# One PSUM tile of two banks for the scores and for the value sums of a unit, with one instruction each for what reads them

## The chip, the cores and the metric

The kernel runs on one core of a Trainium2 chip. The metric is device time in microseconds (us), lower is better. Several runs are made of each kernel and the median is compared. An engine executes its own queue in order: PE is TensorE (matmul), PEld its weight loads, DVE is VectorE, ACT ScalarE, POOL GpSimd, SP the queue that issues most stores and the transposing DMAs. TensorE writes only to PSUM, which has eight banks of 512 fp32 columns; DVE and ACT read it from there.

## The reference

Attention over a sliding window of 32 positions to each side, then a two-layer network with a sigmoid-approximated gelu:

```
scores = (1 / sqrt(64)) * q @ k^T            # q, k, v: (8 batches, 8 heads, 576 positions, 64)
scores = where(|i - j| <= 32, scores, -1e9)
attn   = exp(scores - max) / (sum + 1e-9)
x      = (attn @ v), heads side by side       # 4608 tokens x 512
h      = x @ w_in                             # 512 x 2048
out    = (h * sigmoid(1.702 * h)) @ w_out     # 2048 x 512
```

## The kernel before

**Units and windows.** The 4608 tokens are cut into 36 units of 128. For a unit `u`, `scores(u)` makes transposed scores (keys on partitions, queries on the free axis) of eight heads as two tiles of 128x512, `sc0` for the even heads and `sc1` for the odd ones; each tile is one PSUM bank. Two exponentials (line 277) turn them into the bf16 tile `p`, 128 x (2 x 512). `band(u)` multiplies each half of `p` by a 0/1 mask of the sliding window on DVE (line 288). `values(u)` multiplies `p` (as weights) with `v` and a column of ones, four heads to a bank, so that column 64 of each head is the sum of its exponentials; `norm(u)` then takes, for each bank, four reciprocals (line 310) and one product (line 311) into `x`. `x_T(u)` transposes `x` into `xT`, by a DMA in SP's queue or, in the head, by TensorE.

`layer1(t, d)` does a pair of 128-wide slices of the first layer for two units (256 tokens), eight matmuls into one bank and a gelu on ACT. The second layer is written as seven `product`s of eight matmuls, as in Strassen's method, with sums of `g` (`g_sums`) and of the weights (`w_sums`), and `keep` and `result` moving or adding partial results.

`head()` handles the first seven units with an order of its own. `window(w)` for w = 4 to 17 takes units a = 2w and b = 2w + 1 through attention, layer 1 of the window before, and layer 2 of the window before that. `close()` ends w = 18 and 19. All queues follow the order in which the calls stand (a manual schedule): an instruction placed after another on its engine runs after it.

**PSUM.** All banks come from one pool by tag (`bank`, line 61): "h" has two buffers, "o" one, "t" one, and "a" four, together eight banks. The buffers of a tag are given out in turn; the first write to one waits for the last reader of the tile that held it. "a" serves scores and values, and in the head and in `close` also the transposes `rows_T` and `x_T`, one layer 1 tile, filler matmuls (`keep_busy`) and partial sums of layer 2. `blind(u)` writes an additive mask into the score tiles of units 0 to 3 by matmul, so these need no `band`.

**The part of a window that the change touches** (lines 664 to 672): `product(5)`, `band(a)`, `product(6)`, `band(b, 0)`, `keep(6)`, `band(b, 1)`, one `layer1`, `values(a)`, `values(b)`. On DVE that is: two mask products of a, one of b, the copy of `keep(6)` (line 105, `part<-o_ps`), which waits for `product(6)`, and the second mask product of b. On TensorE: product 5, product 6, eight matmuls of layer 1, 16 matmuls of `values(a)` and 16 of `values(b)`. `norm(a)` and `x_T(a)` follow on DVE and SP.

Of the kernel before, what the change touches and what calls it, by code (L numbers as in the profile page):

```python
# [15 lines left out]
F32 = mybir.dt.float32  # L16
BF16 = mybir.dt.bfloat16
F16 = mybir.dt.float16
AF = mybir.ActivationFunctionType
ALU = mybir.AluOpType  # L20

SQ = 64
# [5 lines left out]
class _Kernel:  # L28
# [30 lines left out]
        self.gs, self.part, self.o_sb = {}, {}, {}  # L59

    def bank(self, kind, shape, dtype, name):
        bufs = {"h": 2, "o": 1, "a": 4, "t": 1}[kind]
        return self.ps.tile(shape, dtype, name=name, tag=kind, bufs=bufs)


    def setup(self):
# [162 lines left out]
    def setup_neg(self):  # L229
# [12 lines left out]
        for rows, b in ((lo, 0), (hi, 1)):  # L242
# [2 lines left out]
            dve.tensor_scalar(out=self.neg[rows, 1 - b, :], in0=tri[0][rows, pad:], scalar1=30000.0, scalar2=-30000.0,  # L245
                              op0=ALU.mult, op1=ALU.add)

    def blind(self, u):

        sc = self.sc[u] = [self.bank("a", [128, 8, SQ], F32, f"sc{eo}") for eo in range(2)]  # L250
        neg = self.neg.rearrange("k (o b) s -> k o b s", o=1).to_broadcast([128, 4, 2, SQ])
        for eo in range(2):
            self.nc.tensor.matmul(sc[eo].rearrange("k (h b) s -> k h b s", b=2), self.ident, neg,
                                  start=True, stop=False, skip_group_check=True)

    def scores(self, u):
        nc = self.nc
        seen = u not in self.sc
        if seen:
            self.sc[u] = [self.bank("a", [128, 8, SQ], F32, f"sc{eo}") for eo in range(2)]  # L260
        sc = self.sc.pop(u)
        k0, q0 = 128 * u % RING, (128 * u + 32) % RING
        for hp in range(4):
            for chunks in ((1, 0), (2,)):
                for eo in range(2):
                    r = slice(eo * 64, eo * 64 + 64)
                    for c in chunks:
                        lo = 64 * (c % 2)
                        b0, n = (1, 1) if c == 2 else (0, 1 + c)
                        nc.tensor.matmul(sc[eo][lo:lo + 64, 2 * hp + b0:2 * hp + b0 + n, :],  # L270
                                         self.kT[r, hp, k0 + 64 * c:k0 + 64 * c + 64],
                                         self.qT[r, hp, q0 + SQ * b0:q0 + SQ * (b0 + n)],
                                         start=(seen and hp == 0 and c < 2), stop=(hp == 3 and c > 0),
                                         skip_group_check=not seen)
        p = self.work.tile([128, 2, 8, SQ], BF16, name="p", tag="p", bufs=5)
        for eo in range(2):
            nc.scalar.activation(p[:, eo], sc[eo], AF.Exp, scale=self.scale)  # L277
        self.p[u] = p

    def band(self, u, only=None):  # L280

        p = self.p[u]
        cross = [(2 * u + i) % 9 == 8 for i in range(2)]
        a, b = 0 if cross[0] else 1, 2 if cross[1] else 3
        for eo in range(2) if only is None else (only,):
            pv = p[:, eo].rearrange("p (h b) s -> p h b s", b=2)
            msk = self.mask[:, a:b + 1:b - a, :].rearrange("p (o b) s -> p o b s", o=1)
            self.nc.vector.tensor_mul(pv, pv, msk.to_broadcast([128, 4, 2, SQ]))  # L288

    def values(self, u, kinds="aa"):  # L290
        nc, D = self.nc, self.D
        p = self.p.pop(u)
        acc = [self.bank(kinds[i], [128, 4, D + 1], F32, f"pv{i}") for i in range(2)]
        for half in range(2):
            for hh in range(4):
                h = 4 * half + hh
                for blk in range(2):
                    vt = (self.ve, self.vo)[blk][u % NV]
                    nc.tensor.matmul(acc[half][blk * 64:blk * 64 + 64, hh, :], p[:, h % 2, h // 2 * 2 + blk, :],  # L299
                                     vt[:, h, :D + 1], start=(hh == 0), stop=(hh == 3))  # L300
        self.acc[u] = acc

    def norm(self, u):
        nc, D = self.nc, self.D
        acc = self.acc.pop(u)
        x = self.work.tile([128, self.H, D], BF16, name="x", tag="x", bufs=4)
        rec = self.work.tile([128, self.H, 1], F32, name="rec", tag="rec", bufs=3)
        for half in range(2):
            hs = slice(4 * half, 4 * half + 4)
            nc.vector.reciprocal(rec[:, hs, :], acc[half][:, :, D:D + 1])  # L310
            nc.vector.tensor_mul(x[:, hs, :], acc[half][:, :, :D], rec[:, hs, :].to_broadcast([128, 4, D]))  # L311
        self.x[u] = x
# [285 lines left out]
    def window(self, w):  # L598
        nc, dve, sp = self.nc, self.nc.vector, self.nc.sync
        a, b = 2 * w, 2 * w + 1  # L600
        att = w < self.NW
        t, act = w - 2, nc.scalar
        l1 = [(lambda d=d: self.layer1(w - 1, d)) for d in range(8)] if w <= self.NW else []

        def run(lst, n=1):
            for _ in range(min(n, len(lst))):
                lst.pop(0)()

        def loads():
            for m in (2 * w + 6, 2 * w + 7):  # L610
                if m < self.NU:
                    self.load_v(m)
            i, chunks = w // 2 + 2, ((0, 1), (2, 3))[w % 2]
            if 512 * i < self.N:
                for c in "kq":
                    self.load_rows(c, i, chunks)

        if w == 4:
            l2 = [(lambda u=u, i=i: self.layer2(u, i, "oh"[u % 2], (dve, act)[u % 2])) for u in (4, 5) for i in range(4)]
            self.scores(7)  # L620
            self.scores(a)
            run(l2, 3)
            self.band(7)
            self.scores(b)
            run(l2)
            self.band(a)
            self.values(7, "th")
            self.gelu_table()
            self.band(b)
            self.norm(7)  # L630
            run(l2, 2)
            self.values(a)
            self.values(b)
            run(l2)
            self.x_T(7, "t", nc.scalar)
            self.norm(a)
            self.x_T(a)
            self.norm(b)
            self.x_T(b)
            run(l2)  # L640
            loads()
            for m in (10, 11):
                self.odd_v(m, dve)
            run(l1, 8)
            self.g_sums(w - 1, 0)
            self.feed(w)
            return
        loads()
        if not att:
            self.close(w, l1)  # L650
            return
        self.scores(a)
        if w > 5:
            self.scores(b)
        self.g_sums(t, 1, (0, 1))
        self.product(t, 1, "o")
        self.keep(t, 1, dve)
        self.product(t, 2, "h")
        if w == 5:
            self.scores(b)  # L660
        self.g_sums(t, 1, (2, 3))
        self.result(t, 11)
        self.gelu_table()
        self.product(t, 5, "t")
        self.band(a)
        self.product(t, 6)
        self.band(b, 0)
        self.keep(t, 6, dve)
        self.band(b, 1)
        run(l1)  # L670
        self.values(a)
        self.values(b)
        self.norm(a)
        self.x_T(a)
        self.product(t, 7)
        self.keep(t, 7, dve)
        self.result(t, 22)
        run(l1, 1)
        self.product(t, 4)
        self.result(t, 21, act)  # L680
        self.norm(b)
        self.x_T(b)
        self.product(t, 3)
        self.result(t, 12)
        run(l1, len(l1) - 4)
        self.g_sums(w - 1, 0)
        self.feed(w)
        run(l1, 4)
# [104 lines left out]
```

The softmax here doesn't subtract the row's maximum and nothing guards it: scores larger than these inputs give would overflow.

## Time and profile before

| | |
|---|---|
| median of four runs | 292.23 us (291.64 to 293.12) |
| the profiled execution | 293.12 us, of which 291.4 us are the span of its instructions |
| busy: PE, DVE, ACT, POOL | 283.5, 192.7, 183.4, 101.8 us |
| granted TensorE clock | 1.0 |
| first-layer matmuls (line 339) | 1152, 134.9 us busy (they overlap) |
| exponentials of 128x512 (line 277) | 72, 604 ns each |
| mask products of 128x512 bf16 (line 288) | 64, 424 ns each |
| reciprocals of 128x4 (line 310) | 72, 174 ns each |
| norm products of 128x256 from PSUM (line 311) | 72, 424 ns each |
| one window in the steady state | 14.57 us |

A line of the table of groups gives the source line, the engine, the operation, output and inputs by their names in the program, the shapes, the count, then the busy time in us and the mean in ns of one; after the second bar stands the idle time of the engine just before such instructions and what ended most of it. A line of the timeline gives start and length in us, then the same names; neighbours of one kind are merged ("x8"). Ends of matmuls are modelled, so that the starts of TensorE's instructions say more than its busy time.

### The profile page before, as it was taken

Reading aid. Unit: us, or ns where it says so; the run is one execution under the profiler, and the core shown is the slowest. Engines: PE = TensorE matmul, PEld = TensorE weight load, DVE = VectorE, ACT = ScalarE, POOL = GpSimd, SP = SyncE. Lnnn points to the kernel's source line nnn. Section 1 sums busy time; section 2 is a strip of 40 time slices with the busy share of each in tenths; the row PEclk is TensorE's granted clock in tenths of the full one; section 3 lists DMA queues with packets and bytes.
Section 4 is the critical chain, followed back from the end, with each engine's and each line's share of the span. In section 5 each row is a group of like instructions: output and inputs, shape, how many; then the busy total and the mean of one; then the engine's idle time right before and its main releaser. Section 6 shows DMA issues by size and latency. Waiting matters only on the chain.

```text
span 291.4 us, 9011 instructions
## 1 busy us (share of the span) xinstructions
PE 283.5 (97%) x3757; PEld 234.0 (80%) x3759; DVE 192.7 (66%) x563; ACT 183.4 (63%) x301; POOL 101.8 (35%) x140
## 2 busy tenths in 40 slices
PE   7979999999999999999999999999999999999995
PEld 3658765866888888888888888888888888888884
DVE  6762467699575858585858585858585858583352
ACT  4566557685766766676767676767676767675330
POOL 8845424998624443433333434332000000000000
PEclk9999999999999999999999999999999999999999
DMA  9999999999999999999999999999935230303012
GB/s 149 180 196 206 199 183 150 172 143 174 177 138 148 156 158 156 144 155 170 134 170 123 155 132 152 141 156 135 158 66 145 38 94 18 97 18 94 2 72 72
DMA packets 144824, 38.79 MB, mean 133 GB/s; under 512 B 129936, under 2 KB 140432, under 8 KB 144784
## 3 DMA queue, kind: packets, MB, share of 16 engines
q0 software_dynamic: 97232, 18.16, 84.6%
q1 hardware_dynamic: 47104, 19.67, 39.1%
q8 instruction: 29, 0.48, 0.7%
q10 hardware_dynamic: 448, 0.39, 0.5%
q14 instruction: 11, 0.09, 0.1%
HBM read 36.96 MB, written 9.44 MB: 159 GB/s over the span
## 4 chain that ended last, share of the span: by engine, by line
PE 88%; DMA 9%; POOL 1%; DVE 1%; issue 0%; ACT 0%; POOLq 0%; DVEq 0%
PE h_ps L339 41%; PE o_ps L401 31%; PE o_ps L351 7%; PE pv L299 4%; PE sc L270 3%; DMA xT<-x 3%; DMA w_in_sb<-in_moe_w_in_dram 3%; DMA ve<-in_v_dram 2%; PE tp L178 1%; POOL ve L159 1%; PE tp L326 0%; DVE o_sb L419 0%; POOL ks L137 0%; POOL qs L137 0%; DVE part L105 0%
## 5 line engine op out<-in xcount | busy, mean ns | idle before, releaser
L339 PE MATMUL h_ps<-xT,w_in_sb 128*128 128x256 bf16 x1152 | 134.9, 273 | 1.3 <-DMA w_in_sb<-in_moe_w_in_dram 1.0
L341 ACT ACTIVATE g<-h_ps 128x512 f16<-128x512 f32 x144 | 85.6, 595 | 74.9 <-PE h_ps L339 73.4
L339 PEld LDWEIGHTS <-w_in_sb 128*128 128x128 bf16 x1152 | 112.1, 98 | 15.1 <-DMA w_in_sb<-in_moe_w_in_dram 1.2
L159 POOL DMA_DIRECT2D ve<-in_v_dram x41 | 34.5, 858 | 82.0 <-PE pv L299 63.6
L401 PEld LDWEIGHTS <-gs 128*128 128x128 f16 x480 | 45.8, 98 | 5.8
L401 PE MATMUL o_ps<-w_sum,gs 128*128 128x256 f16 x360 | 44.3, 273 | 0.0
L277 ACT ACTIVATE p<-sc 128x512 bf16<-128x512 f32 x72 | 37.2, 604 | 3.3 <-PE sc L270 3.1
L378 DVE TENSOR_TENSOR gs<-g 128x512 f16<-128x512 f16 x30 | 12.8, 425 | 38.4 <-ACT g L341 38.4
L401 PEld LDWEIGHTS <-g 128*128 128x128 f16 x360 | 34.2, 98 | 4.5 <-ACT g L341 0.2
L311 DVE TENSOR_TENSOR x<-pv,rec 128x256 bf16<-128x256 f32 x72 | 30.6, 424 | 2.5
L401 PE MATMUL o_ps<-w_out_sb,g 128*128 128x256 f16 x240 | 29.1, 273 | 0.0
L105 DVE COPY vo<-ve 64x528 bf16<-64x528 bf16 x71 | 24.5, 346 | 4.7 <-DMA ve<-in_v_dram 3.1
L105 DVE COPY part<-o_ps 128x256 f32<-128x256 f32 x45 | 19.1, 424 | 12.2 <-PE o_ps L401 11.1
L419 DVE TENSOR_TENSOR o_sb<-o_ps,part 128x256 f32<-128x256 f32 x45 | 19.0, 422 | 12.1 <-PE o_ps L401 11.4
L288 DVE TENSOR_TENSOR p<-p,mask 128x512 bf16<-128x512 bf16 x64 | 24.6, 424 | 0.0
L147 POOL DMA_DIRECT2D qs<-in_q_dram x27 | 23.2, 885 | 3.6 <-DMA ks<-in_k_dram 1.7
L351 PE MATMUL o_ps<-w_out_sb,g 128*128 128x512 f16 x96 | 23.2, 380 | 0.0
L147 POOL DMA_DIRECT2D ks<-in_k_dram x27 | 23.0, 882 | 0.3 <-issue 0.3
L438 ACT ACT_TABLE_LOAD x15 | 19.2, 1283 | 0.3
L277 ACT ACT_TABLE_LOAD x15 | 19.2, 1283 | 0.3
L310 DVE RECIPROCAL rec<-pv 128x4 f32<-128x4 f32 x72 | 12.5, 174 | 7.6 <-PE pv L299 7.6
L299 PEld LDWEIGHTS <-p 128*64 128x64 bf16 x576 | 11.1, 110 | 5.9 <-DVE p L288 2.9
(79 smaller groups left out, 237.9 us busy)
## 6 DMA issues: line engine op xcount, KB each, us to landing
out_dram<-o_sb SPq DMA_DIRECT2D x34, 256.0 KB, 2.8
ve<-in_v_dram POOLq DMA_DIRECT2D x31, 128.0 KB, 5.7
ks<-in_k_dram POOLq DMA_DIRECT2D x24, 128.0 KB, 6.8
qs<-in_q_dram POOLq DMA_DIRECT2D x24, 128.0 KB, 8.8
w_in_sb<-in_moe_w_in_dram POOLq DMA_DIRECT2D x4, 512.0 KB, 9.9
w_out_sb<-in_moe_w_out_dram POOLq DMA_DIRECT2D x4, 512.0 KB, 14.2
ve<-in_v_dram POOLq DMA_DIRECT2D x10, 64.0 KB, 5.8
ks<-in_k_dram POOLq DMA_DIRECT2D x7, 64.0 KB, 5.6
```

Of the source, the lines that this page charges most:

```text
L105: (eng.copy if eng is self.nc.scalar else eng.tensor_copy)(out, in_)
L147: self.nc.gpsimd.dma_start(self.stage[key][off:off + m, n], src[b, :, s:s + m, :].rearrange("h s d -> s h d"))
L159: self.nc.gpsimd.dma_start(self.ve[m % NV][lo + off:lo + off + n, :, :self.D], self.v[b, :, s:s + n, :].rearrange("h s d -> s h d"))
L277: nc.scalar.activation(p[:, eo], sc[eo], AF.Exp, scale=self.scale)
L288: self.nc.vector.tensor_mul(pv, pv, msk.to_broadcast([128, 4, 2, SQ]))
L299: nc.tensor.matmul(acc[half][blk * 64:blk * 64 + 64, hh, :], p[:, h % 2, h // 2 * 2 + blk, :], vt[:, h, :D + 1], start=(hh == 0), stop=(hh ...
L311: nc.vector.tensor_mul(x[:, hs, :], acc[half][:, :, :D], rec[:, hs, :].to_broadcast([128, 4, D]))
L339: nc.tensor.matmul(hps[:, i, :], self.w_in_sb[:, kr, ff * 128:(ff + 1) * 128], self.xT[t][:, kr, :], start=(i == 0 and kr == 0), stop=(i = ...
L341: nc.scalar.activation(self.g[t][:, ffs[0]:ffs[1] + 1:ffs[1] - ffs[0], :], hps, AF.Gelu_apprx_sigmoid)
L351: nc.tensor.matmul(o_ps, self.g[t][:, ff, s * 128:(s + 1) * 128], self.w_out_sb[:, ff, :], start=(ff == 0), stop=(ff == self.NFF - 1))
L401: nc.tensor.matmul(self.part[t, key], x, y, start=(first and k == 0), stop=(k == 7), skip_group_check=True)
L438: self.nc.scalar.activation(self.spark, self.spark, AF.Gelu_apprx_sigmoid)
```

## The change

The tag "a" gets two buffers of two banks each (`two_banks`). `bank("a", ...)` still serves the one-bank users, which now get the first bank of such a buffer. The two score tiles of a unit become the two halves of one tile, and so do the two value tiles (except `values(0)`, `values(1)` and `values(7)`, which take banks of other tags by name and keep the old form). The exponential runs once over 1024 columns, the mask product once over 1024, the reciprocal once over eight columns and the norm product once over 512. In `window` the two halves of `band(b)` around `keep(6)` become one `band(b)` after it. The matmuls are the same ones in the same order.

```diff
     def bank(self, kind, shape, dtype, name):
-        bufs = {"h": 2, "o": 1, "a": 4, "t": 1}[kind]
-        return self.ps.tile(shape, dtype, name=name, tag=kind, bufs=bufs)
+        if kind == "a":
+            n = 1
+            for d in shape[1:]:
+                n *= d
+            flat = self.two_banks(name, dtype)[:, 0, :n]
+            dims = "abc"[:len(shape) - 1]
+            return flat.rearrange(f"p ({' '.join(dims)}) -> p {' '.join(dims)}", **dict(zip(dims, shape[1:])))
+        return self.ps.tile(shape, dtype, name=name, tag=kind, bufs={"h": 2, "o": 1, "t": 1}[kind])
+
+    def two_banks(self, name, dtype=F32):
+        return self.ps.tile([128, 2, 512 if dtype == F32 else 1024], dtype, name=name, tag="a", bufs=2)
...
+    def score_banks(self):
+        return self.two_banks("sc").rearrange("k e (h s) -> k e h s", s=SQ)
...
         p = self.work.tile([128, 2, 8, SQ], BF16, name="p", tag="p", bufs=5)
-        for eo in range(2):
-            nc.scalar.activation(p[:, eo], sc[eo], AF.Exp, scale=self.scale)
+        nc.scalar.activation(p, sc, AF.Exp, scale=self.scale)
         self.p[u] = p
 
-    def band(self, u, only=None):
+    def band(self, u):
...
-        for eo in range(2) if only is None else (only,):
-            pv = p[:, eo].rearrange("p (h b) s -> p h b s", b=2)
-            msk = self.mask[:, a:b + 1:b - a, :].rearrange("p (o b) s -> p o b s", o=1)
-            self.nc.vector.tensor_mul(pv, pv, msk.to_broadcast([128, 4, 2, SQ]))
-
-    def values(self, u, kinds="aa"):
+        pv = p.rearrange("p e (h b) s -> p (e h) b s", b=2)
+        msk = self.mask[:, a:b + 1:b - a, :].rearrange("p (o b) s -> p o b s", o=1)
+        self.nc.vector.tensor_mul(pv, pv, msk.to_broadcast([128, 8, 2, SQ]))
+
+    def values(self, u, kinds=None):
...
-        acc = [self.bank(kinds[i], [128, 4, D + 1], F32, f"pv{i}") for i in range(2)]
+        if kinds is None:
+            both = self.two_banks("pv")[:, :, :4 * (D + 1)].rearrange("q i (h d) -> q i h d", d=D + 1)
+            acc, self.acc[u] = [both[:, i] for i in range(2)], [both]
+        else:
+            acc = self.acc[u] = [self.bank(kinds[i], [128, 4, D + 1], F32, f"pv{i}") for i in range(2)]
...
+        if len(acc) == 1:
+            rec4 = rec.rearrange("q (i h) o -> q i h o", i=2)
+            nc.vector.reciprocal(rec4, acc[0][:, :, :, D:D + 1])
+            nc.vector.tensor_mul(x.rearrange("q (i h) d -> q i h d", i=2), acc[0][:, :, :, :D],
+                                 rec4.to_broadcast([128, 2, 4, D]))
+            self.x[u] = x
+            return
...
         self.product(t, 5, "t")
         self.band(a)
         self.product(t, 6)
-        self.band(b, 0)
         self.keep(t, 6, dve)
-        self.band(b, 1)
+        self.band(b)
         run(l1)
         self.values(a)
         self.values(b)
```

More of the change, by code (lines that the diff above doesn't have):

```diff
@@ L246, in setup_neg @@
                               op0=ALU.mult, op1=ALU.add)
+    def score_banks(self):
+        return self.two_banks("sc").rearrange("k e (h s) -> k e h s", s=SQ)
     def blind(self, u):
-        sc = self.sc[u] = [self.bank("a", [128, 8, SQ], F32, f"sc{eo}") for eo in range(2)]
+        sc = self.sc[u] = self.score_banks()
         neg = self.neg.rearrange("k (o b) s -> k o b s", o=1).to_broadcast([128, 4, 2, SQ])
         for eo in range(2):
-            self.nc.tensor.matmul(sc[eo].rearrange("k (h b) s -> k h b s", b=2), self.ident, neg,
+            self.nc.tensor.matmul(sc[:, eo].rearrange("k (h b) s -> k h b s", b=2), self.ident, neg,
                                   start=True, stop=False, skip_group_check=True)
@@ L259, in scores @@
         if seen:
-            self.sc[u] = [self.bank("a", [128, 8, SQ], F32, f"sc{eo}") for eo in range(2)]
+            self.sc[u] = self.score_banks()
         sc = self.sc.pop(u)
@@ L269, in scores @@
                         b0, n = (1, 1) if c == 2 else (0, 1 + c)
-                        nc.tensor.matmul(sc[eo][lo:lo + 64, 2 * hp + b0:2 * hp + b0 + n, :],
+                        nc.tensor.matmul(sc[lo:lo + 64, eo, 2 * hp + b0:2 * hp + b0 + n, :],
                                          self.kT[r, hp, k0 + 64 * c:k0 + 64 * c + 64],
@@ L300, in values @@
                                      vt[:, h, :D + 1], start=(hh == 0), stop=(hh == 3))
-        self.acc[u] = acc
     def norm(self, u):
```

## The prediction

> **What bounds the kernel now.** I read the page first (busy shares, then the chain of waits), then TensorE's own waits, then a table of three windows, then one window in order of time.
>
> ```profile
> span 291.4 us, 9011 instructions
> PE 283.5 (97%) x3757; PEld 234.0 (80%) x3759; DVE 192.7 (66%) x563; ACT 183.4 (63%) x301; POOL 101.8 (35%) x140
> ...
> PE 88%; DMA 9%; POOL 1%; DVE 1%; issue 0%; ACT 0%; POOLq 0%; DVEq 0%
> ```
>
> TensorE ends the chain for 88% of the span. DVE and ACT, the engines whose instructions the change merges, have about 1% between them. TensorE's busy time is modelled, so 97% alone would not prove that it is full. Its waits and a window do:
>
> ```profile
> PE h_ps L339 <- DMA w_in_sb<-in_moe_w_in_dram: 1.0, 1, 1.0
> PE tp L326 <- DVE x L311: 0.6, 2, 0.4
> ...
> PE h_ps L339 <- DMA xT<-x: 0.3, 1, 0.3
> ```
>
> ```profile
> 187.60:202.17 14.57, 14.57 (x202) 12.74 (x201) 10.15 (x30) 9.87 (x16) 5.25 (x7) 1.00 1.85 146
> ```
>
> The second answer gives, after start and length, the busy time of PE, PEld, DVE, ACT and POOL. PE is busy for 14.57 of 14.57 us at a full granted clock; DVE has 4.4 us to spare and ACT 4.7. From 22.3 us to the last product TensorE is late once: near 111.9 us layer 1 waits for a transposing DMA of x (by the starts of its matmuls 0.61 us from one to the next, where 0.11 is usual, so 0.5 us). So the change can gain only what TensorE waits today, and lose wherever it makes TensorE wait.
>
> **What the Trainium skill says.** "VectorE: DVE Perf Modes", section "The TRN2 errata", says that Vector and Scalar operations pay a fixed cost per instruction, once for a large tile and once each for small ones; that is the saving meant here. "Advanced Engine Details and Errata", section "The Read-Write Bubble", adds that one instruction may read several PSUM banks. The trace agrees with the first (rows below); no run here yet shows a two-bank read. "TensorE: Matmul & The Clock Gate", Part 2, says that matmuls stay in program order and only weight loads are pulled ahead: so one late weight load of `p` holds everything behind it.
>
> **The change, part by part.** Durations:
>
> ```profile
> L277 ACT ACTIVATE p<-sc 128x512 bf16<-128x512 f32 x72 | 37.2, 604 | 3.3 <-PE sc L270 3.1
> L311 DVE TENSOR_TENSOR x<-pv,rec 128x256 bf16<-128x256 f32 x72 | 30.6, 424 | 2.5
> L288 DVE TENSOR_TENSOR p<-p,mask 128x512 bf16<-128x512 bf16 x64 | 24.6, 424 | 0.0
> L310 DVE RECIPROCAL rec<-pv 128x4 f32<-128x4 f32 x72 | 12.5, 174 | 7.6 <-PE pv L299 7.6
> ...
> L366 DVE TENSOR_TENSOR w_sum<-w_out_sb,w_sum 128x1024 f16<-128x1024 f16 x4 | 2.8, 688 | 2.0 <-DMA w_out_sb<-in_moe_w_out_dram 2.0
> ```
>
> 1. Exponential. ACT copies of 320 and 512 columns take 424 and 583 ns, so a column costs 0.83 ns, and one of 1024 columns takes 604 + 512 x 0.83, about 1.03 us. Four in a row take 2.06 us now (they overlap by some 90 ns), two would take about 1.9. Gain on ACT: about 0.15 us a window, beside TensorE, which does products then: worth 0. The first half no longer arrives early, but values() of a window start 3 us after the exponentials begin.
>
> 2. Mask product. The row w_sum has 1024 two-byte elements; in the timeline one takes 0.68 us (at 54.24 and 58.36). So 0.68 in place of 0.42 + 0.34 (the start-to-start step) = 0.76. Gain on DVE 0.08 a unit; worth 0, but it decides item 5.
>
> 3. Reciprocal and norm product: now 0.17, 0.42, 0.17, 0.42 with starts 0.22 and 0.34 apart, about 1.2 us a unit. After: about 0.18, then 0.69 (copies of 512 fp32 columns out of PSUM take 687 ns), 0.9 in all. Gain about 0.3 a unit on DVE. norm(b) ends earlier, but x_T(b) stands in SP's queue behind the store of result 21 (store at 189.88, transpose at 190.42 against a norm that ends at 189.71), so the one late transpose, itself such an x_T(b) issued at 102.23, isn't issued earlier: worth 0.
>
> 4. Buffers. Four one-bank buffers become two of two banks. In the windows scores, scores, values, values took two banks each in turn already, so each tile waits for the same predecessor. In the head one-bank users now fill a whole buffer: the eight rows_T tiles of tokens 512 to 1023 have two buffers in place of four. A k tile is copied out at 37.63 + 0.69 = 38.32, and the next k tile's transposes begin at 38.45: 0.07 us in hand after a hand-over of 0.06 (item 5). The later ones, 0.14; the q copies on ACT, 0.2 and more. Worth 0; if a hand-over were 0.1 later, under 0.2 us in all. values(5) needs norm(4): mask, reciprocal and product end near 48.1, its start is near 48.3. Blind, x_T and close() have their predecessors done long before.
>
> 5. The edit in window(). band(b, 0), keep(6), band(b, 1) becomes keep(6), band(b). That moves half of b's mask product behind keep(6), which waits for product 6:
>
> ```profile
> 185.05 1.04 PE L339 MATMUL h_ps<-xT,w_in_sb 128*128 128x256 bf16 x8
> ...
> 185.25 0.42 DVE L105 COPY part<-o_ps 128x256 f32<-128x256 f32 x1 [0.19 <-PE o_ps L401]
> 185.59 0.42 DVE L288 TENSOR_TENSOR p<-p,mask 128x512 bf16<-128x512 bf16 x1
> 186.01 0.59 PEld L299 LDWEIGHTS <-p 128*64 128x64 bf16 x32 [0.21 <-DVE p L288]
> ```
>
> The 0.21 us before the weight loads is no wait for DVE, though it is named: scores have the same 0.21 with "issue" as cause; it is the switch to half-width tiles. Of the 32 loads the first 16 are unit a, the other 16 unit b. They start (0.59 - 0.11) / 31 = 0.0155 us apart, so b's first is at 186.01 + 0.25 = 186.26. Its mask is ready now at 186.01. After: 185.59 + 0.68 = 186.27. From the end of a DVE result to the weight load that needs it:
>
> ```profile
> 18.90 0.42 DVE L311 TENSOR_TENSOR x<-pv,rec 128x256 bf16<-128x256 f32 x1
> ...
> 19.38 0.11 PEld L326 LDWEIGHTS <-x 128*128 128x128 bf16 x2 [0.47 <-DVE x L311]
> ```
>
> 19.38 - 19.32 = 0.06. So b's first load can start at 186.33 in place of 186.26, 0.06 to 0.07 late, and values(b), then product 7 and all of TensorE wait behind it. The offsets between keep(6) and values are the same in every window (0.76) except the one delayed by the transpose. There are 13 such windows, w = 5 to 17: 12 x 0.06 = 0.7 us. Bounds for one window: 0 (the load ran 0.03 ahead of its matmul, and a little of the rest may be hidden) and 0.17 (a restart that also exposes one weight load of 0.11). I take 0.06, since restarts after a wait in the head show load and matmul at the same time.
>
> 6. Removed waits on TensorE. Its built queue has 470 rows with a wait in place of 558. In values(a) the third matmul starts 0.05 after the first and later pairs are 0.03 apart; values(b), with the same waits, shows 0.03 there too (186.33 to 186.36). So satisfied waits cost nothing and their removal is worth 0. In window 4 values(7) now waits for the second half of its mask; the whole one ends about 0.05 earlier: -0.05.
>
> **Sum.** +0.7 - 0.05, about +0.65 us. The profiled execution took 293.12, 1.7 around its span; the median of the four runs is 292.23. The sum is a difference, so it goes onto the median: 292.9 us.
>
> **Rivals.** (B) The late load is hidden after all: the pull-ahead absorbs it, or DVE starts band(b) sooner. Then nothing on TensorE changes: 292.2. For it: the margin is a few hundredths. Against: program order behind one load.
>
> (C) Slower. Same place, a larger price: each restart of values(b) exposes the weight load, 0.17 x 12 = 2.0 us, or the 1024-element mask with its repeated operand runs longer than the w_sum row. 294.2. It decides once the wait passes 1.46 / 12 = 0.12 us a window. For it: the start of values is already unhidden, and one half mask in the head took 0.82 us, with POOL copies beside it. Against: the 0.06 of the restarts seen, and no POOL copies in the windows.
>
> (D) Faster. The 88 waits gone from TensorE are each worth the 0.02 us of that first pair: 1.8 us, 290.4. For it: TensorE is full, so anything per instruction counts at once. Against: the second unit's pair.
>
> **How the numbers follow.** What can be told from no change here is about 0.5%, 1.46 us. Chances: forecast 0.55, B 0.12, C 0.22, D 0.11. So within 0.5%: 0.67; slower 0.22; faster 0.11. The range takes the forecast's bounds (0 to 1.5 us) with the runs' own scatter (291.64 to 293.12) and reaches into C: 291.4 to 294.4.
>
> **What would show it.** Right: in a window the weight loads of p split into 16 and 16 with a gap of some 0.06 named for DVE, the window 14.63 in place of 14.57, DVE busy about 0.7 us less a window. Wrong: windows still at 14.57 with band(b) ending before the load (B); windows of 14.7 and more (C); shorter than 14.57 (D); or new waits for tp copies between 37 and 43 us, which I hold to be covered.

## The result, and the profile after

| | before | after |
|---|---|---|
| median of the runs compared | 292.34 us (54 runs, 291.04 to 294.15) | 293.23 us (33 runs, 292.27 to 295.15) |
| the profiled execution | 293.12 us, span 291.4 | 292.62 us, span 290.9 |

The ratio of after to before is 1.0032, with an interval of 1.0020 to 1.0043: 0.94 us slower (0.58 to 1.26). Forecast was +0.65. The two profiled executions stand the other way round, by 0.5 us. They are one sample each, and differ where the change has no part. In that of before a chunk of `w_in` landed late (TensorE waited 1.0 us) and a transposing DMA held layer 1 for 0.5 us; the one of after has neither wait. So what the change does is read from single windows and rows, and its size from the medians.

The page of after, first its span and busy times, then the shares of the chain of waits:

```profile
span 290.9 us, 8877 instructions
PE 283.0 (97%) x3757; PEld 234.4 (81%) x3759; DVE 182.6 (63%) x465; ACT 181.1 (62%) x265; POOL 101.5 (35%) x140
...
PE 93%; DMA 3%; DVE 1%; ACT 1%; POOL 0%; issue 0%; POOLq 0%; DVEq 0%
```

DVE has 98 instructions and 10.1 us of busy time less, ACT 36 and 2.3 us less. TensorE has the same number of matmuls and still ends the chain. The groups of after, from the table of lines (busy us and mean ns of one behind the first bar):

```profile
L288 ACT ACTIVATE p<-sc 128x1024 bf16<-128x1024 f32 x36 | 34.9, 1021 | 3.4 <-PE sc L282 3.2
...
L324 DVE TENSOR_TENSOR x<-pv,rec 128x512 bf16<-128x512 f32 x33 | 22.8, 691 | 1.1
L298 DVE TENSOR_TENSOR p<-p,mask 128x1024 bf16<-128x1024 bf16 x32 | 21.7, 684 | 0.1
...
L323 DVE RECIPROCAL rec<-pv 128x8 f32<-128x8 f32 x33 | 6.7, 202 | 5.5 <-PE pv L313 5.5
```

All four are what was worked out from the rows of before: 1021 ns (1.03 us), 691 (0.69), 684 (0.68), 202 (0.18). The first line also shows one instruction reading two PSUM banks, as the Trainium skill has it ("Advanced Engine Details and Errata", "The Read-Write Bubble"); the trace of before could not show that.

None of this saving reaches TensorE, and each window is longer. The answer for one window gives start and end, length, busy PE, PEld, DVE, ACT and POOL, granted clock, DMA share, GB/s:

```profile
199.17:213.80 14.63, 14.63 (x202) 12.81 (x202) 9.59 (x25) 9.74 (x15) 1.76 (x2) 1.00 0.84 117
```

DVE is busy 9.59 us where it was 10.15, ACT 9.74 where it was 9.87, and the window takes 14.63 us where it took 14.57. Measured from the weight load that begins one unit a's values to the next one, it is 14.630 in place of 14.575. The timeline at the start of that window shows where the difference comes from:

```profile
198.20 1.04 PE L359 MATMUL h_ps<-xT,w_in_sb 128*128 128x256 bf16 x8
198.40 0.42 DVE L114 COPY part<-o_ps 128x256 f32<-128x256 f32 x1 [0.57 <-PE o_ps L421]
198.74 0.68 DVE L298 TENSOR_TENSOR p<-p,mask 128x1024 bf16<-128x1024 bf16 x1
199.17 0.65 PEld L313 LDWEIGHTS <-p 128*64 128x64 bf16 x32 [0.21 <-issue]
...
199.42 0.19 PE L313 MATMUL pv<-ve,p 128*64 128x65 bf16 x1
199.48 0.22 PE L313 MATMUL pv<-ve,p 128*64 128x65 bf16 x1
199.53 0.20 PE L313 MATMUL pv<-ve,p 128*64 128x65 bf16 x1
```

The mask product of b now stands whole behind `keep(6)`, runs from 198.74 and ends at 199.42. The loads of `p` (32, of which the first 16 are unit a) begin at 199.17; b's first starts at 199.48, 0.06 after the mask ends. The 32 loads take 0.65 us where they took 0.59. The first matmul of b is 0.06 us behind the last of a, and the next 0.05 behind that, where 0.03 is usual: TensorE restarts after a short stop. From a's first weight load to b's is 0.312 us (0.253 before), in all 13 windows. The label on the load line names only what came ahead of its first load, so a wait inside a merged line has to be read from its length and from the starts.

### The profile page after: what moved, and what is told of

It is laid out like the page before. It is cut to its first block, busy times and chain, and to the rows that moved or that the text cites. A ratio compares the mean times of both kernels' runs of the same rounds, so it can differ in the third digit from the quotient of the medians.

```text
span 290.9 us, 8877 instructions
## 1 busy us (share of the span) xinstructions
PE 283.0 (97%) x3757; PEld 234.4 (81%) x3759; DVE 182.6 (63%) x465; ACT 181.1 (62%) x265; POOL 101.5 (35%) x140
## 4 chain that ended last, share of the span: by engine, by line
PE 93%; DMA 3%; DVE 1%; ACT 1%; POOL 0%; issue 0%; POOLq 0%; DVEq 0%
PE h_ps L359 43%; PE o_ps L421 32%; PE o_ps L371 6%; PE pv L313 4%; PE sc L282 4%; DMA qs<-in_q_dram 2%; DMA ve<-in_v_dram 2%; PE tp L187 1%; PE tp L346 1%; PE tp L216 1%; PE sc L265 0%; ACT p L288 0%; DVE o_sb L439 0%; POOL ks L146 0%; PE junk L464 0%
## 5 line engine op out<-in xcount | busy, mean ns | idle before, releaser
L288 ACT ACTIVATE p<-sc 128x1024 bf16<-128x1024 f32 x36 | 34.9, 1021 | 3.4 <-PE sc L282 3.2
L324 DVE TENSOR_TENSOR x<-pv,rec 128x512 bf16<-128x512 f32 x33 | 22.8, 691 | 1.1
L298 DVE TENSOR_TENSOR p<-p,mask 128x1024 bf16<-128x1024 bf16 x32 | 21.7, 684 | 0.1
L313 PEld LDWEIGHTS <-p 128*64 128x64 bf16 x576 | 11.7, 110 | 6.3 <-issue 2.9
L421 PE MATMUL o_ps<-w_sum,g 128*128 128x256 f16 x120 | 15.6, 273 | 0.0
```

What stands on the lines that cost most here:

```text
L288: nc.scalar.activation(p, sc, AF.Exp, scale=self.scale)
L298: self.nc.vector.tensor_mul(pv, pv, msk.to_broadcast([128, 8, 2, SQ]))
L324: nc.vector.tensor_mul(x.rearrange("q (i h) d -> q i h d", i=2), acc[0][:, :, :, :D], rec4.to_broadcast([128, 2, 4, D]))
L421: nc.tensor.matmul(self.part[t, key], x, y, start=(first and k == 0), stop=(k == 7), skip_group_check=True)
```

## The experiments

Theory A is that of the prediction: this late weight load is the loss, whatever the merging itself does. Against it stands theory B, that the loss comes with the two-bank tiles or the merged instructions and not with that order. Each run's ratio is to runs of the kernel before on the same chip; 1% is 2.92 us. e4 and e6 have four runs each, the others 14 to 22.

**Undo the order alone.** The changed kernel, with `band` able to do one half again:

```diff
         self.product(t, 6)
+        self.band(b, 0)
         self.keep(t, 6, dve)
-        self.band(b)
+        self.band(b, 1)
```

> The changed kernel with one part undone: band(b) is again two halves around keep(6); two-bank tiles, single exponential, reciprocal and norm product stay. Theory A (late mask of unit b): the second half of the mask ends 0.26 us earlier, the 0.06 us stop before values(b) goes, the window is 14.57 us again, and the time is 0.7 us under the changed kernel: about +0.2 us against before. Theory B (the loss comes from two buffers in place of four, or from two-bank reads, not from the window's order): stays at +0.9 us against before.

Measured: 0.9999 (0.9981 to 1.0018), windows 14.575 us, 0.252 us from a's first load to b's. In the timeline of this kernel:

```profile
198.09 0.42 DVE L114 COPY part<-o_ps 128x256 f32<-128x256 f32 x1
198.43 0.41 DVE L299 TENSOR_TENSOR p<-p,mask 128x512 bf16<-128x512 bf16 x1
198.86 0.59 PEld L318 LDWEIGHTS <-p 128*64 128x64 bf16 x32 [0.21 <-DVE p L299]
```

The half mask ends at 198.84, ahead of the loads, and the 32 loads are back at 0.59 us. Everything else of the change is in this kernel, and its windows are those of before: A holds, B falls.

**The other way to take the wait away.** The whole mask ahead of `keep(6)`:

```diff
         self.product(t, 6)
-        self.keep(t, 6, dve)
         self.band(b)
+        self.keep(t, 6, dve)
```

> The changed kernel with the whole band(b) ahead of keep(6) in place of behind it. Theory A: the mask ends about 0.7 us before the weight load that needs it, keep(6) comes about 0.3 us later and nobody waits for it; window 14.57 us, about +0.2 us against before, as with the split. Theory B: +0.9 us, as the changed kernel.

Measured: 1.0013 (0.9996 to 1.0030), windows 14.575 us.

```profile
197.65 0.69 DVE L298 TENSOR_TENSOR p<-p,mask 128x1024 bf16<-128x1024 bf16 x1 [0.22 <-ACT p L288]
198.26 0.42 DVE L114 COPY part<-o_ps 128x256 f32<-128x256 f32 x1
198.76 0.59 PEld L313 LDWEIGHTS <-p 128*64 128x64 bf16 x32 [0.21 <-DVE part L114]
```

The mask is done 0.42 us before the loads. The label of the load names `part`, which no load of `p` reads: it is the last DVE event before it, and the 0.21 us are the same with any name. `keep(6)` comes 0.26 us later here and nobody waits for it.

**The order without the change.** In the kernel before, with its one-bank tiles and its halves, `keep(6)` is put ahead of both halves of the mask:

```diff
         self.product(t, 6)
-        self.band(b, 0)
         self.keep(t, 6, dve)
+        self.band(b, 0)
         self.band(b, 1)
```

> The kernel before with one part of the change alone: both half masks of unit b behind keep(6), all tiles of one bank. Theory A: the second half ends 0.342 + 0.342 + 0.416 = 1.10 us after keep(6) starts, the load that needs it (the third of unit b) could go at 1.05 and goes at 1.155: 0.10 us a window, 13 windows, +1.4 us against before. Theory B: no change against before.

Measured: 1.0041 (1.0023 to 1.0059), +1.2 us; windows 14.668 us, +0.093 (but for the one whose values come late behind a transposing DMA, where the mask is in time).

```profile
213.86 0.42 DVE L105 COPY part<-o_ps 128x256 f32<-128x256 f32 x1 [0.53 <-PE o_ps L401]
214.20 0.75 DVE L288 TENSOR_TENSOR p<-p,mask 128x512 bf16<-128x512 bf16 x2
214.62 0.68 PEld L299 LDWEIGHTS <-p 128*64 128x64 bf16 x32 [0.21 <-DVE p L288]
```

The same loss without any merged instruction, and larger, as two halves in a row take 0.75 us and one whole 0.68: 13 x 0.093 is 1.2 us. So the merged mask product does save its 0.07 us a unit. Since only the third load of b needs the second half here, 0.03 us after the first, 0.04 of that shows: the changed kernel loses 0.055 a window and not 0.093.

**A larger dose.** The changed kernel, with the first half of b's mask multiplied once more behind it (it is 0 and 1, so the output stays):

```diff
         self.keep(t, 6, dve)
         self.band(b)
+        self.band(b, 0)
```

> The changed kernel with a redundant mask product of the first half of unit b (multiplying by 0 or 1 twice changes nothing) right behind band(b): a larger dose of the same delay. It starts some 0.04 us after band(b) ends and takes 0.42, so the weight load comes 0.45 us later than in the changed kernel. Theory A: 0.45 x 13 = 5.9 us over the changed kernel, +6.8 us against before. Theory B: DVE has over 4 us to spare in a window, so no change against the changed kernel: +0.9 us.

Measured: 1.0267 (1.0229 to 1.0305), +7.8 us, where 6.8 was expected; windows 15.135 us, +0.56 over the kernel before and 0.505 over the changed one (0.45 expected).

```profile
188.56 0.68 DVE L303 TENSOR_TENSOR p<-p,mask 128x1024 bf16<-128x1024 bf16 x1
188.99 0.33 PEld L318 LDWEIGHTS <-p 128*64 128x64 bf16 x16 [0.21 <-issue]
...
189.28 0.42 DVE L299 TENSOR_TENSOR p<-p,mask 128x512 bf16<-128x512 bf16 x1
...
189.77 0.36 PEld L318 LDWEIGHTS <-p 128*64 128x64 bf16 x16 [0.45 <-ACT spark L463]
```

The wait is now long enough to cut the 32 loads into 16 and 16, and b's 16 start at 189.77, 0.07 after the extra mask ends (the name after it is not its cause). At the usual 0.25 us after a's first load they were due at 189.24, so they are 0.53 late, and the window is 0.56 longer: each window pays the lateness in full, and no matmul goes ahead meanwhile. That is what the Trainium skill says ("TensorE: Matmul & The Clock Gate", Part 2: matmuls stay in order). 13 x 0.56 is 7.3 of the 7.8.

**Is the merged norm worth anything?** The kernel of e2 with the reciprocals and norm products by halves, on the same two-bank tiles:

```diff
         if len(acc) == 1:
-            rec4 = rec.rearrange("q (i h) o -> q i h o", i=2)
...
-            self.x[u] = x
-            return
+            acc = [acc[0][:, i] for i in range(2)]
```

> The kernel with band(b) ahead of keep(6), and also the norm by halves again (two reciprocals and two products per unit), so that of the merged instructions only the exponential and the mask product are left. Theory A (DVE's and ACT's savings are beside TensorE): windows stay at 14.57 us although DVE is some 0.5 us busier in each; in the head x_T(2), which TensorE does wait for, has its last transposes about 0.2 us later after values(2) than with one product; time within 0.5 us of before. Theory C (the merged norm shortens the path and pays for part of the loss): windows longer than 14.57.

Measured: 1.0038 (1.0020 to 1.0057), +1.1 us, where at most 0.5 either way was expected; windows 14.575 us, so the windows do not have it. In its profile one window (the "second" of the texts below: from the values of w = 6 to those of w = 7, at 97.94 us in the kernel before) waits 0.4 us for a transposing DMA of `x`, as in the kernel before. That raised the question taken up by e10 to e12.

**Cover for the late mask.** The changed kernel with product 7 between the two units, so that b's mask has a microsecond more:

```diff
         self.values(a)
-        self.values(b)
...
         self.product(t, 7)
+        self.values(b)
```

(`norm(a)` and `x_T(a)` stay behind `values(a)`.)

> The changed kernel with product 7 put between values(a) and values(b), so that the mask of unit b has 0.9 us more. Theory A: the 0.06 us stop goes, but TensorE changes between wide and half-width tiles once more: by the starts of before 0.126 + 0.202 + 0.126 in place of 0.031 + 0.126 + 0.109, and 0.02 for the slower first pair, so +0.21 us; window 14.78 us against 14.63 in the changed kernel, 13 windows, +2.0 us over it, about +2.8 against before. Theory D (the changes of tile width cost nothing by themselves): window 14.57, +0.2 against before.

Measured: 1.0101 (1.0067 to 1.0136), +2.95 us; windows 14.80 us. The wait for the mask is gone, and more is lost, as the expectation had it; theory D falls:

```profile
185.70 0.33 PEld L313 LDWEIGHTS <-p 128*64 128x64 bf16 x16 [0.21 <-issue]
186.07 0.77 PEld L421 LDWEIGHTS <-gs 128*128 128x128 f16 x8
187.05 0.33 PEld L313 LDWEIGHTS <-p 128*64 128x64 bf16 x16 [0.21 <-issue]
```

Both groups of half-width loads have the 0.21 us in front of them. From the last full-width matmul to the first half-width one it is 0.203 us by the starts (0.109 between full-width ones), back again 0.127 and 0.120. Keeping a and b together pays that once a window: against the 14.575 of e2 the second switch costs 0.225.

**The tail.** In e1 and e2 the windows are those of before, and yet the traces show something left over. From the start of the last matmul to the end of the execution, 3.83 us pass in the kernel before and 4.44 in the changed one. The DMA view of the last 5.5 us, of the kernel before:

```profile
q1 hardware_dynamic: 368, 0.33, 19.8%
q10 hardware_dynamic: 96, 0.07, 4.9%
...
out_dram<-o_sb SPq DMA_DIRECT2D x1, 128.0 KB, 1.7
```

and of the changed kernel (queue: packets, MB, share; then issues with KB and us to landing):

```profile
q1 hardware_dynamic: 368, 0.33, 19.8%
q10 hardware_dynamic: 96, 0.07, 4.9%
q14 instruction: 1, 0.01, 0.8%
...
out_dram<-o_sb SPq DMA_DIRECT2D x1, 128.0 KB, 2.5
```

One packet of the instruction queue (8 KB, at 287.8 us, on a DMA engine for 0.73 us) lies among the last stores, and SP's last one lands after 2.5 us in place of 1.7. The changed ScalarE program is 36 instructions shorter, so its last block may be fetched at another time. To test it, three kernels execute `gelu_table`'s one-element activation twice, 15 ScalarE instructions more and nothing on TensorE:

```diff
-        self.nc.scalar.activation(self.spark, self.spark, AF.Gelu_apprx_sigmoid)
+        for _ in range(2):
+            self.nc.scalar.activation(self.spark, self.spark, AF.Gelu_apprx_sigmoid)
```

> The run with the merged mask product ahead of keep(6) (e2_ahead), with gelu_table's one-element activation executed twice, which adds 15 instructions to ScalarE's program and nothing to TensorE's. In all kernels with the merged exponentials an 8 KB packet of the instruction queue falls among the last output stores, and 4.3 to 4.5 us pass from the start of the last matmul to the end of the execution; in the kernel before no such packet lies there and 3.8 us pass. Theory E (the packet delays the last stores): ScalarE's last fetch comes some 13 us earlier, out of the tail; from the last matmul's start to the end 3.85 us; windows 14.575 us as in e2_ahead; time within 0.2 us of the kernel before, with e8 and e9 to compare it with. Theory F (the longer tail comes from something else in the changed kernel, such as its tiles): the tail stays at 4.3 to 4.5 us and the time 0.4 to 0.6 us above the kernel before.

> The changed kernel with the same second one-element activation in gelu_table. Theory E: windows 14.63 us as in the changed kernel, from the last matmul's start to the end 3.85 us in place of 4.4, so the price of the windows alone is left: +0.7 us against the kernel before, where the changed kernel has +0.9. Theory F: tail 4.4 us, +0.9 to +1.3.

> Control: the kernel before with the same second one-element activation. Windows 14.575 us, and within 0.2 us of the kernel before, if the 15 further activations lie in ScalarE's idle time. Both theories expect this, as long as none of ScalarE's fetches moves into the tail: before has its fetches near 55, 147 and 250 us, and with 15 further instructions the last comes earlier.

Measured: e7 1.0009 (0.9989 to 1.0029), e8 1.0020 (1.0004 to 1.0036), and the control e9 0.9992 (0.9975 to 1.0010): the second activation costs nothing that can be measured. The same view of e8:

```profile
q1 hardware_dynamic: 368, 0.33, 19.9%
q10 hardware_dynamic: 96, 0.07, 4.9%
...
out_dram<-o_sb SPq DMA_DIRECT2D x1, 128.0 KB, 1.7
```

The packet is gone (it now comes near 268.7 us, 19 us earlier) and the store lands after 1.7 us again (SP issues it, so it was no wait of ScalarE for its program); from the last matmul to the end it is 3.83 us in e7 and e8, while e8's windows stay at 14.63. Over all profiles of this study the six with a packet there (after, e1, e2, e4, e5, e6) have 4.31 to 4.49 us, the eight without 3.83 to 3.87. The six are those whose ScalarE program is 36 instructions shorter than that of before; the number on DVE does not matter (e5 has the packet; e11, with ScalarE's program of before, has not). That the fetch lengthens the tail is shown for the profiled executions. What it costs without a profile is not measured as well: after over e8 is 0.35 us, e2 over e7 0.1, e5 over e10 (below) 1.1, a mean of 0.5, but each of the three is uncertain by 0.6 to 0.8, and e1, which has the packet too, measured no loss.

**The transposing DMA.** Up to e9 every profile with the norm by halves (before, e3, e5, e9) had the wait for the second transpose of `x` in the second window, and every one with the merged norm (seven) had none. Two kernels take the norm alone: e10 is e7 with the norm by halves (the edit of e5); e11 is e1 with the exponentials by halves too, so that only the two-bank tiles, the merged reciprocal and the norm product are left of the change. e12 is e7 once more beside them.

```diff
-        nc.scalar.activation(p, sc, AF.Exp, scale=self.scale)
+        for eo in range(2):
+            nc.scalar.activation(p[:, eo], sc[:, eo], AF.Exp, scale=self.scale)
```

> e7_ahead_two_sparks (merged exponential and mask, keep(6) behind band(b), ScalarE's last fetch out of the tail) with the reciprocals and norm products by halves as in the kernel before. In the four profiles so far that have the norm by halves, layer 1 waits 0.1 to 0.5 us in the second window for the second transposing DMA of x, which lands 9.3 to 9.7 us after its issue; in the seven with the merged norm it lands after 7.3 to 9.0 us and nothing waits. Theory G (the merged norm brings that landing earlier and takes the wait away): the second transpose lands 9.3 us or more after its issue, the second window is 0.1 to 0.5 us longer, and the time is 0.2 to 0.5 us above e7. Theory H (the landing scatters from execution to execution, whatever the norm): no second window longer than 14.63, or the time within 0.2 us of e7's.

> The changed kernel with the exponentials and mask products by halves again, and band(b, 0), keep(6), band(b, 1) in window(): of the change only the two-bank tiles, the merged reciprocal and the merged norm product are left. Windows 14.575 us; ScalarE's program is that of the kernel before, so no fetch in the tail, and 3.85 us from the last matmul's start to the end. Theory G: no wait for the transposing DMA in the second window, and 0.2 to 0.5 us under the kernel before. Theory H: as the kernel before, within 0.2 us.

> e7_ahead_two_sparks again, on the chip and in the rounds of e10 and e11, since 0.2 to 0.5 us are to be told apart. Both theories: second window 14.575 us, tail 3.85 us. Theory G: 0.2 to 0.5 us under e10 and within 0.2 us of e11. Theory H: within 0.2 us of both.

Measured: e10 0.9999 (0.9981 to 1.0016), e11 1.0006 (0.9991 to 1.0021), e12 1.0008 (0.9990 to 1.0025). The wait is in e11 and e12, with the merged norm; of e11, then of e12:

```profile
PE h_ps L361 <- DMA xT<-x: 0.6, 1, 0.6
```

```profile
PE h_ps L359 <- DMA xT<-x: 0.5, 1, 0.5
```

and it is missing in e10, with halves. Eleven profiles had split cleanly and the next three all went the other way. e7 and e12 are even the same kernel: the second transpose lands after 7.56 us in the profile of one and after 9.82 in that of the other. The transposes are issued at the same place in the window (4.29 to 4.34 us after `values` in before, after, e5, e7), and land 7.5 to 9.9 us later as the execution has it: theory H. The merged norm is worth nothing that can be measured here, alone (e11 against before) or with the rest (e7 and e12 against e10); an effect under about 0.7 us could still hide in the intervals. With the halves e10 is not slower than e7 or e12, so e5's +1.1 us is not the price of halves. e5's profile has the packet in its tail (0.5 us) and that wait (0.4 us, but the profile of before has it too); what makes up e5's +1.1 us stays open.

No version was faster than the kernel before.

## Why the prediction was right

- **What bounds the kernel.** Confirmed: 2.3 us less on ACT and 10.1 us less on DVE shortened no window (e2 keeps the 2.3 and 9.7 of the 10.1, and its windows take 14.575 us).
- **Items 1 to 3.** The durations came out within 0.02 us. Two exponentials in a row take 1.94 us (1.9). DVE's busy time fell by 0.55 us a window where about 0.7 was expected: the 1.2 us of a unit's norm contained short gaps, which are not busy time. Worth 0, as said; e11 and e10 show it for the norm from both sides. The transposing DMA is issued where it was, as item 3 argued.
- **Item 4, buffers.** In the profile of the changed kernel the transposes of 35 to 40 us run at the same spacing as before (1.31 us between two k tiles). That does not hold in every execution: in e4, e5, e6 and e8, all with the two-bank pool, DVE's first copy out of `tp` came later, behind the casts of q rows that had landed late. In e5 that copy (`kT<-tp`) runs from 36.39 to 37.07, and the second k tile starts at 37.12, 1.42 us after the first. So the margin of 0.07 that the item had in hand was used up, and the smaller number of buffers cost 0.11 us in these four, inside the 0.2 that it allowed for. None of the three profiles with four buffers (before, e3, e9) shows it.
- **Item 5, the edit in `window`.** This is the loss. Predicted 0.06 us a window and 0.7 in all; measured 0.055 and, over 13 windows, 0.72. The step that found it was to compare the end of the merged mask with the start of the load that reads it. The 0.06 from a DVE result to the load, read from one restart in the head, held in every window (0.054 to 0.055). e1 and e2 take the loss away, e3 makes it alone, e4 enlarges it. One of the signs named did not come: the loads stayed a single row of 32, longer by 0.06 us and labelled "issue", and only e4's larger dose split them.
- **Item 6.** In window 4 `values(7)` does wait for the end of its mask in most profiles of both kinds: by the starts 0.1 us in the kernel before (so TensorE was late there too, beside the one place that the prediction counts), 0.5 in e9, 0.3 in the changed kernel, and not at all in e3, e6 and e10. It depends on when DVE has finished the copies of `v` ahead of it. Where it is awaited, two halves take 0.74 us and the whole one 0.67; the gain of about 0.05 is worked out from that, and no median shows it.
- **The rivals.** B of the prediction (a hidden load) is excluded by the windows. C needed 0.12 us a window; the restart cost no more than the lateness. D fell: e1, e2 and e11, which keep the merged instructions or part of them, are not faster than before.
- **What was not in the sum.** The tail, 0.6 us in the profiled execution, is a term of the forecast's size that no step looked for. The windows and it make 1.3 us, just over the upper end of the measured 0.58 to 1.26; e8, which has the windows alone, measured +0.58 (0.12 to 1.05) for their 0.72. So the windows are shown to cost what was predicted, and the total is known no better than these intervals. That the whole forecast of +0.65 still lies inside the measured interval is in part luck: a term about as large as itself was left out, and it counts less in the medians, if at all, than in the profiles.

## What to carry to other kernels

TensorE was full here, so merging instructions on other engines gained nothing by itself, and the order that the merge forced was what counted: a half that used to be ready early becomes ready with the whole. Compare the end of the merged instruction with the start of the first weight load that reads it, to a hundredth of a microsecond: in this loop, without slack on TensorE, a lateness of 0.055 us was paid in each of 13 windows. When several profiles agree with a cause that nobody has varied, vary it before believing it.

## What the runs showed of the hardware

- A change of ScalarE's instruction count moves a fetch of its program: 8 KB through the DMA engines that also carry the stores. Among the last stores it put 0.4 to 0.7 us on the end of the profiled execution (six profiles against eight); 15 one-element activations moved it out.
- A change from full-width to half-width weights on TensorE took 0.203 us from start to start in e6, about 0.09 beyond the usual 0.109, and a little more on the way back (0.127 and 0.120); e6 paid 0.225 us for one more pair of changes.
- The landing of the same transposing DMA, issued at the same point of the window, varied between 7.5 and 9.9 us from one profile to another (7.56 and 9.82 in two of one kernel, e7 and e12), enough for waits of 0 to 0.75 us on a window.
- From the end of a DVE result to the weight load that waits for it: 0.053 to 0.055 us in all 13 windows of the changed kernel and of e8, 0.07 behind the longer wait of e4.
